# State copies moved ahead of a unit's loads, four plain items in place of two, partial sums added on VectorE

## The chip, the core and the metric

The kernel runs on one core of a Trainium2 chip: TensorE (PE), VectorE (DVE), ScalarE (ACT), GpSimd (POOL) and SyncE (SP), with 16 DMA engines. Its time is the device time of one execution in microseconds (us); a comparison uses the median of several.

## The reference

Two stages, all in float32 on the chip. First an mLSTM cell over `batch, heads, seq, head_dim = 4, 8, 768, 40`, then a two-layer block with tanh shrink (3072 tokens, 320 features, 2048 hidden):

```python
for t in range(S):
    m_new = np.maximum(f_gate[:, :, t] + m, i_gate[:, :, t])
    f_stab = np.exp(f_gate[:, :, t] + m - m_new);  i_stab = np.exp(i_gate[:, :, t] - m_new)
    C = f_stab * C + i_stab * outer(v_t, k_t);     n = f_stab * n + i_stab * k_t
    y[t] = sigmoid(o_gate[t]) * (C @ q_t) / np.maximum(np.abs(n @ q_t), 1.0)
x = y.transpose(0, 2, 1, 3).reshape(3072, 320)
h = x @ w_in            # 320 x 2048
out = (h - np.tanh(h)) @ w_out   # 2048 x 320
```

`w_in` and `w_out` arrive as 64-bit floats and are converted to float32 on the chip.

## The kernel before

**Units.** The cell works in 24 units of 128 tokens (4 batches, 6 chunks; unit `n` is chunk `n // 4` of batch `n % 4`). For a unit, `load_unit` fetches `kz`, `qz`, `v`, `k` and `o` through SP's queue. Units 0 to 5 are done in a first part whose order a planner (`Plan`, `plan_unit`, `plan_weights`) works out when the program is built; the conversion of the weights runs through it too (the first DVE operation of a weight block is a shift, `w_e<-w`; the list `begun` keeps these shifts in order). In this part TensorE fills its gaps with `awake` matmuls on a constant.

**Second part.** From unit 6 (`PLANNED`) on, each batch keeps its state in another layout, in halves; `in_halves(b)` makes it from the old one with seven small copies on SP's queue (`state<-state` in the profile). `block_turned` computes a unit's output transposed (`pT`), `turn_back` sends it through DRAM (`h_rows<-zt`, then `z_in<-h_rows`, both on SP's queue), and `gate_turned` gates it on DVE (`den<-z_in`, `o<-o,den`, two `ys`); `turn_by_store` turns it into the block's input (`yt`, `y_rows`, `xT`). `cell_slot` lays these steps out over two items for each unit, and at its begin issues the loads of the unit that follows.

**Items.** The two-layer block works on groups of 256 tokens (12 groups) times pairs of hidden blocks (8 for each group, `p`). An *item* is two pairs of one group. Its first product (`ph_up`) is computed either plainly (`up`: 8 matmuls of 128x128 by 256 columns, and the last 64 features) or with seven block products in place of eight (`up_in_seven`: 14 matmuls of 128 columns, copies of partial sums on ACT, sums of the weights from `sum_w_in`, sums of x from `sum_x`). The sums of the weights of pairs 0 to 3 lie where the partial outputs `part` of groups 0 to 2 lay. The polynomial in place of `h - tanh(h)` follows: squares on ACT (`z`, `q`), the rest on DVE (`gt<-ph_up,z`, `gt<-q,gt`). The two PSUM banks of `ph_up` are free for the next item when DVE has read them in `gt<-ph_up,z`. The second product (`pS`, 14 matmuls for each item, on sums `s` of `gt` and `wT` of w_out) lags one item: six of the 14 are held over and, in an item done in seven, are set between the stages of its first product. At a group's end `put_together(g)` adds the seven results (`a` on ACT, `ob`, `u` on DVE), and the next group's `pS` needs the banks it reads.

The planned part ends with item 6. Items 7 and 8 (group 0, pairs 4 to 7) are plain, items 9 and 10 (group 1) and 11 and 12 (group 2) are done in seven, as are all of groups 3 to 11 from item 13 on, but for the last. Groups 0 to 2 had their pairs 0 to 3 in the planned part; these are the `part` sums that `put_together` adds for `g < FIRST` (3).

**Order.** Every engine runs its instructions in the order in which they are written, and SP, ACT and POOL issue DMAs in that order as well. In the second part `merge` walks through an item's TensorE steps and puts the other steps in by their place (a number such as START + 2.33: a third of the way through the third item from START, item 7); `Clock.later` delays some of them. A `pause` in `cell_slot` is an empty step that moves the steps behind it later; a slot of unit pairs has 21 steps.

Of the kernel before, what the change touches and what calls it, by code (L numbers as in the profile page):

```python
# [55 lines left out]
OP = mybir.AluOpType  # L56
# [23 lines left out]
def kernel(  # L80
# [33 lines left out]
    V, A, SP, G = Pinned(nc.vector), Pinned(nc.scalar), Pinned(nc.sync), Pinned(nc.gpsimd)  # L114
# [168 lines left out]
    NG = NU // GT  # L283
    NP = NFF // 2
# [9 lines left out]
    FIRST, SPLIT = 3, 4  # L294
    NX = 6
    PLANNED, LEFT = 6, 3
# [58 lines left out]
    def load_unit(n, names=("kz", "qz", "v", "k", "o", "q2"), queue=SP, behind=(), crossed=False):  # L355
        c, b = divmod(n, B)
        t = ld.setdefault(n, {})
        t["crossed"] = crossed
        for name in names:
            if crossed and (name == "v" or name == "k" and n + B < NU):  # L360
                whole = load.tile([L, H if name == "v" else WIDE, D], FP, name=name, tag=name, bufs=3)
                t[name] = whole
                if name == "k":
                    G.memset(whole[:, H:], 0.0)
                load_crossed(whole[:, 0:H], (v if name == "v" else k)[b, c])
            elif name in ("kz", "qz"):
                t[name] = load.tile([128, HH, L], FP, name=name, tag=name, bufs=3)
                for i in range(2):
                    src = kT if name == "kz" else qT
                    dma = queue.dma_start(out=t[name][i * HALF:i * HALF + D], in_=src[b, c, :, i * HH:(i + 1) * HH])  # L370
                    if behind:
                        tc.add_manual_dep(dma.ins, behind[-1].ins.name, SYNC, reason="order of transfers")
            elif name == "k":
                if n + B < NU:
                    t["k"] = load.tile([L, WIDE, D], FP, name="k", tag="k", bufs=3)
                    queue.dma_start(out=t["k"].rearrange("p h d -> p (h d)"),
                                    in_=bass.AP(k.tensor, k[b, c].offset, [[H * D, L], [1, WIDE * D]]))
            elif name != "q2":
                src, bufs = {"v": (v, 3), "o": (o_gate, 4)}[name]
                t[name] = load.tile([L, H, D], FP, name=name, tag=name, bufs=bufs)  # L380
                queue.dma_start(out=t[name], in_=src[b, c])
            elif c:
                first = (n + 2) % 3 * len(TRIOS) * L
                t["q2"] = sums_in[0:TOP].rearrange("p a b -> p (a b)")[:, first:first + len(TRIOS) * L].rearrange("p (j t) -> p j t", t=L)
                for i in range(TRIO):
                    queue.dma_start(out=t["q2"][i * D:(i + 1) * D, 0:len(range(i, H, TRIO))], in_=qT[b, c, :, slice(i, H, TRIO)])
# [20 lines left out]
    two = const.tile([128, 1], FP, name="two")  # L407
# [30 lines left out]


    CHUNKS = (0, 2, NT)  # L440
    NS = NG * NP + 2 + (NG - FIRST) * NP // 2 - 1 + LEFT * (NP - SPLIT) // 2 - 2
    NW = NS + len(CHUNKS) - 1
    sums = const.tile([128, NW + 4 * NP], FP, name="sums")

# [10 lines left out]
    crossed = const.tile([L, NT - NEW, BH], FP, name="crossed")  # L455
# [17 lines left out]
    begun = []  # L473
# [24 lines left out]
    def gate_columns(c0, c1, bank):  # L498

        cs = slice(c0, c1)  # L500
        some = CHUNKS.index(c0)
        least = sums[:, NS + some:NS + some + 1]

# [137 lines left out]
    parts_of = [const.tile([L, GT, DM], FP, name=f"part{g}") for g in range(NP // 2)]  # L641
# [207 lines left out]
    def in_halves(b):  # L849


        c = NEW + (b < PLANNED % B)
        old, new = (state[b][(c + i) % 2].rearrange("p h d -> p (h d)") for i in (0, 1))
        for h in (0, 1, 2, 4, 5, 6, 7):
            i, j = divmod(h, HH)
            r = h % TRIO
            n = 2 if h == 0 else 1
            to, at = (x[:, first * D1:(first + TRIO * (n - 1) + 1) * D1].rearrange("p (h d) -> p h d", d=D1)[:, ::TRIO]
                      for x, first in ((new, j), (old, h)))
            SP.dma_start(out=to[i * HALF:i * HALF + D], in_=at[r * D:(r + 1) * D])  # L860
# [93 lines left out]
    def cell_slot(s, o):  # L954


        steps, pause = [], [(0.0, lambda: None)]
        if s is not None:
            if s + 1 < NU and s + 1 not in ld:
                load_unit(s + 1, ("kz", "qz", "v", "k", "o"), crossed=True)  # L960
            begin(s)
        def ready():
            prepare(s)
            G.memset(un[s]["wide"][:, H * D1:], 0.0)

        if o is None:
            return [(0.0, ready)]
        steps += 5 * pause
        if s is not None:
            steps.append((0.0, ready))  # L970
        steps += 5 * pause
        gates, behind = [], 5 * pause if o > PLANNED else 2 * pause
        if o == PLANNED:
            steps += 3 * pause
        steps.append((0.0, lambda: [gates.extend(gate_turned(o)), gates[0]()]))
        steps += [(0.0, lambda i=i: gates[i]()) for i in range(1, 4)]
        steps.append((0.0, lambda: turn_by_store(o)))
        return steps + behind
# [7 lines left out]
    gS, wT, pS, third = {}, {}, {}, {}  # L986
# [9 lines left out]
    def order_of(g):  # L996

        half = NP // 2
        return [0, half - 1, *range(half, NP), *range(1, half - 1)] if g == FIRST else list(range(NP))
# [72 lines left out]
    def put_together(g):  # L1072
        bank = pS[g]

        ob = mlp.tile([128, 5, HM], FP, name="ob", tag="ob")
        a = mlp.tile([128, HM], FP, name="a", tag="a", bufs=1)
        u = mlp.tile([128, 2, HM], FP, name="u", tag="u", bufs=1)

        def twice(t):
            return t.unsqueeze(1).to_broadcast([128, 2, HM])  # L1080

        def rest():
            V.tensor_tensor(out=ob[:, 0:5:4], in0=bank[0][:, 0:2], in1=twice(a), op=OP.add)
            V.tensor_tensor(out=u, in0=bank[1], in1=twice(ob[:, 4]), op=OP.add)
            V.tensor_tensor(out=ob[:, 3], in0=bank[1][:, 0], in1=u[:, 1], op=OP.add)
            V.tensor_tensor(out=ob[:, 1:3], in0=bank[2], in1=u, op=OP.add)
            if g < FIRST:
                both = ob[:, 0:2 * GT]
                (V if g in third else G).tensor_tensor(out=both, in0=both, in1=parts_of[g].rearrange("p t (two n) -> p (t two) n", two=2), op=OP.add)
            c, b = divmod(g * GT, B)  # L1090
            rows = out.rearrange("(b c t) n -> c t b n", b=B, c=NT)[c][:, b:b + GT]
            whole = ob[:, 0:4].rearrange("p (t two) n -> p t (two n)", two=2)
            if g >= FIRST or g in third:
                Clock.later("sent", 2.0, lambda: A.dma_start(out=rows, in_=whole))
            else:
                G.dma_start(out=rows, in_=whole)

        if g in third:
            return lambda: A.copy(out=a, in_=bank[0][:, 2]), rest
        A.copy(out=a, in_=bank[0][:, 2])  # L1100
        Clock.later("result", 0.5, rest)
# [301 lines left out]
    while sum(map(len, items)) < len(pairs):  # L1403
        x = sum(map(len, items))
# [11 lines left out]
    HOLD = 161.0478  # L1416
    FETCH = {(0, 1): 0.0000, (2, 1): 0.0000, (3, 0): 26.0323, (3, 1): 0.0000}
    APART = ()
    PLAIN = 2
    assert 3 * len(items) - START - PLAIN - 1 == NS  # L1420
    BETWEEN = 3
    BY_POOL = (1, 2, 3, 5, 6, 7,)
# [46 lines left out]
    of_tokens, of_states, exponentials, rows = {}, {}, [], []  # L1469
# [266 lines left out]
    for i, slot in enumerate(slots):  # L1736
        x0, x1 = (START + max(0, 2 * j - 1) for j in (i, i + 1))
        begins[x0].append((slot, x0, x1))
    for p, x in enumerate((4.05, 6.05, 8.05, 2.8, 0.5, 0.8, 1.1, 1.4)):
        spread_over([(0.0, lambda step=step: step()) for step in sum_w_in(p, G)], START + x, START + x + 0.25)  # L1740
    late = (4, 0.0, V), (5, 0.04, G), (6, 0.95, V), (7, 0.3, G)
    for p, x, E in (*late, *((p, x, G) for p, x in zip(order_of(FIRST)[:2] + order_of(FIRST)[-2:], (2.3, 2.7, 6.6, 7.5)))):
        spread_over([(0.0, lambda p=p, i=i, E=E: sums_at(p, E)[i][1]()) for i in range(4)], START + x, START + x + (0.1 if E is V else 0.3))
    for g, x in (1, 0.1), (2, 2.1):
        spread_over([(0.0, lambda g=g: sum_x(g, V))], START + x, START + x + 0.1)
    banks[:] = [name for name in ("b0", "b1") if name != third.setdefault("tag", "b0")]
    cross()
    load_unit(PLANNED, ("kz", "qz", "v", "k", "o"), crossed=True)
    in_halves(PLANNED % B)
    in_halves((PLANNED + 1) % B)  # L1750
    load_unit(PLANNED + 1, ("kz", "qz", "v", "k", "o"), crossed=True)
    in_halves((PLANNED + 3) % B)
# [148 lines left out]
    with tc.If(loaded[0] > 0):  # L1901
# [21 lines left out]
        for g in range(NG):  # L1923
# [30 lines left out]
            for tt in range(GT):  # L1954
                o = mlp.tile([128, 5, HM], FP, name="ob", tag="ob")[:, 0:2].rearrange("p two n -> p (two n)")
# [43 lines left out]
```

## Time and profile before

| | |
|---|---|
| Runs | 497.73, 501.45, 504.31 us; median 501.45 |
| The profiled execution | 498.91 us, of which the span from first to last instruction is 497.2 |
| Busy in the span | PE 97%, DVE 83%, ACT 54%, POOL 26% |
| Granted TensorE clock, mean | 0.997 |

The page gives busy times and groups of instructions; a timeline row is start, duration, engine, operation, tiles, count, and in brackets how long the engine sat idle before it and what ended that. A row of several instructions counts to the last one's end; a float32 matmul of this program stands as two records. Rows of the SP queue are the issue of DMAs, not their transfer.

### The profile page before, as it was taken

How to read it: one execution, taken by the hardware profiler on the slowest of the kernel's cores; microseconds unless marked ns; L12 is line 12 of the kernel's file. 1: busy time of each engine (PE TensorE's matmuls, PEld its weight loads, DVE VectorE, ACT ScalarE, POOL GpSimd, SP SyncE). 2: the span in 40 equal slices, each digit the busy share in tenths (PEclk: the TensorE clock that was granted, in tenths of full speed). 3: DMA queues.
4: the chain of work that ended last, by engine and by line, in shares of the span. 5: the costliest groups of instructions: out<-in, count | busy, mean ns of one | idle time of the engine just before them, and what ended most of it. 6: DMA issues, size and time to landing. Idle time of an engine off the chain costs nothing.

```text
span 497.2 us, 13817 instructions
## 1 busy us (share of the span) xinstructions
PE 483.0 (97%) x5208; PEld 432.8 (87%) x5208; DVE 411.2 (83%) x963; ACT 268.8 (54%) x729; POOL 129.0 (26%) x246
## 2 busy tenths in 40 slices
PE   9999999999999999999999999999999999999993
PEld 5778876788878999999999999999999999989983
DVE  4898979996999998997988888887887988776771
ACT  4888968634444544644644644644554644645440
POOL 5642325910735542111111111102102111111000
PEclk9999999999999999999999999999999999999998
DMA  7995494222634435545544444434525532410001
GB/s 224 297 263 181 74 203 139 73 69 46 122 92 120 88 92 114 114 90 118 107 95 102 96 105 106 93 91 109 101 67 113 110 82 38 90 37 1 26 2 32
DMA packets 143468, 51.26 MB, mean 103 GB/s; under 512 B 124004, under 2 KB 135716, under 8 KB 143396
## 3 DMA queue, kind: packets, MB, share of 16 engines
q1 hardware_dynamic: 135308, 31.70, 31.3%
q0 software_dynamic: 5424, 15.51, 10.5%
q10 hardware_dynamic: 2664, 3.11, 1.8%
q8 instruction: 43, 0.70, 0.6%
q14 instruction: 29, 0.24, 0.2%
HBM read 38.40 MB, written 11.60 MB: 101 GB/s over the span
## 4 chain that ended last, share of the span: by engine, by line
PE 60%; DVE 1%; issue 0%; ACT 0%
PE ph_up L129 27%; PE pS L129 27%; PE pT L129 3%; PE ps L129 2%; PE pc L129 1%; DVE gt L106 0%; DVE s L106 0%; DVE ob L106 0%; ACT ph_up L106 0%; DVE both L106 0%; DVE ys L106 0%; DVE u L106 0%; DVE yt L106 0%; PE count L129 0%
## 5 line engine op out<-in xcount | busy, mean ns | idle before, releaser
L129 PE MATMUL ph_up<-xT,w_in 64*64 64x256 f32 (+3 forms) x1324 | 155.0, 349 | 0.0
L129 PEld LDWEIGHTS ph_up<-xT,w_in 128*128 128x128 f32 (+2 forms) x1324 | 113.9, 162 | 17.2 <-issue 3.5
L106 ACT ACTIVATE z<-ph_up 128x256 f32<-128x256 f32 (+1 forms) x98 | 40.8, 417 | 106.1 <-PE ph_up L129 86.1
L106 POOL DMA_DIRECT2D xT<-y_rows x54 | 31.7, 592 | 230.5 <-DMA y_rows<-yt 230.5
L106 ACT COPY ph_up<-ph_up 128x256 f32<-128x256 f32 x117 | 41.9, 358 | 85.5 <-PE ph_up L129 54.7
L129 PE MATMUL pS<-wT,s 128*128 128x160 f32 x504 | 86.7, 300 | 0.0
L129 PEld LDWEIGHTS pS<-wT,s 128*128 128x128 f32 x504 | 72.9, 191 | 0.3 <-issue 0.3
L106 DVE SCALAR_TENSOR_TENSOR gt<-q,gt 128x512 f32<-128x512 f32 (+1 forms) x98 | 66.6, 686 | 4.6 <-ACT q L106 2.0
L106 ACT ACTIVATE q<-z,tiny 128x512 f32<-128x512 f32 (+1 forms) x98 | 68.9, 713 | 2.5
L106 DVE TENSOR_TENSOR both<-ph_up,cs 128x256 f32<-128x256 f32 x78 | 31.9, 419 | 30.8 <-PE ph_up L129 26.6
L129 PE MATMUL pS<-w_out,gt 128*128 128x160 f32 x336 | 56.9, 312 | 0.0
L129 PE MATMUL ph_up<-xT,sums_in 128*128 128x128 f32 x336 | 52.3, 278 | 3.6 <-DVE gt L106 3.0
L129 PEld LDWEIGHTS pS<-w_out,gt 128*128 128x128 f32 x336 | 46.8, 189 | 4.4 <-issue 1.9
L129 PEld LDWEIGHTS ph_up<-xT,sums_in 128*128 128x128 f32 x336 | 45.3, 191 | 6.0 <-issue 4.1
L129 PE MATMUL ph_up<-xT,part 128*128 128x128 f32 x288 | 44.9, 278 | 0.4 <-POOL ob L106 0.3
L106 DVE SCALAR_TENSOR_TENSOR gt<-ph_up,z 128x256 f32<-128x256 f32 (+1 forms) x98 | 41.1, 456 | 2.3 <-ACT z L106 2.2
L129 PEld LDWEIGHTS ph_up<-xT,part 128*128 128x128 f32 x288 | 38.8, 191 | 2.6 <-ACT ph_up L106 1.9
L106 DVE TENSOR_TENSOR s<-gt 128x256 f32<-128x256 f32 x84 | 33.6, 439 | 1.4
L129 PE MATMUL pS<-w_out,s 128*128 128x160 f32 x168 | 29.7, 299 | 0.0
L129 PE MATMUL pS<-wT,gt 128*128 128x160 f32 x168 | 29.7, 299 | 0.0
L129 PE MATMUL po<-w_out,gt 128*128 128x320 f32 x96 | 28.2, 440 | 1.2 <-DVE part L106 1.2
L106 DVE SCALAR_TENSOR_TENSOR gt<-both,z 128x512 f32<-128x512 f32 x39 | 29.3, 751 | 0.0
(140 smaller groups left out, 741.9 us busy)
## 6 DMA issues: line engine op xcount, KB each, us to landing
w<-in_moe_w_out POOLq DMA_DIRECT2D x8, 640.0 KB, 6.9
h_rows<-zt SPq DMA_DIRECT2D x72, 64.0 KB
z_in<-h_rows SPq DMA_DIRECT2D x72, 64.0 KB
w<-in_moe_w_in POOLq DMA_DIRECT2D x16, 256.0 KB, 6.3
kz<-in_kT SPq DMA_DIRECT2D x48, 80.0 KB
o<-in_o_gate SPq DMA_DIRECT2D x24, 160.0 KB
qz<-in_qT SPq DMA_DIRECT2D x44, 80.0 KB
y_rows<-yt SPq DMA_DIRECT2D x68, 40.0 KB
```

The costliest lines, as they stand in the source:

```text
L106: i = method(*args, **kwargs)
L129: return cls.keep(nc.tensor.matmul(*args, **kwargs))
```

## The change

1. `in_halves(2)` (seven copies) is issued ahead of the loads of unit 6, not behind them; and the `kz` and `qz` loads of unit 6 wait for the fourth-last shift of the weights (`behind=begun[-4:-3]`).
2. The gate steps of unit 6 move two of 21 steps later in their slot (START + 2.33 to START + 2.52).
3. `PLAIN` is 4, not 2: items 9 and 10 use `up`, and `sum_x(1)` is not needed. Two columns of `sums` fewer.
4. The sums of weights on POOL are made at other places; two sets of `wT` come earlier.
5. For groups 0 to 2 the addition of `part` in `put_together` runs on DVE in place of POOL, and the result is sent from ACT's queue, not POOL's.

```diff
-    NS = NG * NP + 2 + (NG - FIRST) * NP // 2 - 1 + LEFT * (NP - SPLIT) // 2 - 2
+    NS = NG * NP + 2 + (NG - FIRST) * NP // 2 - 1 + LEFT * (NP - SPLIT) // 2 - 4
...
-        gates, behind = [], 5 * pause if o > PLANNED else 2 * pause
+        gates, behind = [], 5 * pause if o > PLANNED else []
         if o == PLANNED:
-            steps += 3 * pause
+            steps += 5 * pause
...
-                (V if g in third else G).tensor_tensor(out=both, in0=both, in1=parts_of[g]..., op=OP.add)
+                V.tensor_tensor(out=both, in0=both, in1=parts_of[g]..., op=OP.add)
...
-            if g >= FIRST or g in third:
-                Clock.later("sent", 2.0, lambda: A.dma_start(out=rows, in_=whole))
-            else:
-                G.dma_start(out=rows, in_=whole)
+            Clock.later("sent", 2.0, lambda: A.dma_start(out=rows, in_=whole))
...
-    PLAIN = 2
+    PLAIN = 4
...
-    for p, x in enumerate((4.05, 6.05, 8.05, 2.8, 0.5, 0.8, 1.1, 1.4)):
+    for p, x in enumerate((4.05, 6.05, 8.05, 2.02, 1.2, 1.5, 2.2, 2.45)):
         spread_over([... for step in sum_w_in(p, G)], START + x, START + x + 0.25)
-    for p, x, E in (*late, *((p, x, G) for p, x in zip(order_of(FIRST)[:2] + order_of(FIRST)[-2:], (2.3, 2.7, 6.6, 7.5)))):
+    for p, x, E in (*late, *((p, x, G) for p, x in zip(order_of(FIRST)[:2] + order_of(FIRST)[-2:], (0.7, 0.95, 6.6, 7.5)))):
...
-    for g, x in (1, 0.1), (2, 2.1):
+    for g, x in ((2, 2.1),):
         spread_over([(0.0, lambda g=g: sum_x(g, V))], START + x, START + x + 0.1)
     cross()
-    load_unit(PLANNED, ("kz", "qz", "v", "k", "o"), crossed=True)
     in_halves(PLANNED % B)
+    load_unit(PLANNED, ("kz", "qz", "v", "k", "o"), behind=begun[-4:-3], crossed=True)
     in_halves((PLANNED + 1) % B)
```

More of the change, by code (lines that the diff above doesn't have):

```diff
@@ L1088, in rest @@
                 both = ob[:, 0:2 * GT]
-                (V if g in third else G).tensor_tensor(out=both, in0=both, in1=parts_of[g].rearrange("p t (two n) -> p (t two) n", two=2), op=OP.add)
+                V.tensor_tensor(out=both, in0=both, in1=parts_of[g].rearrange("p t (two n) -> p (t two) n", two=2), op=OP.add)
             c, b = divmod(g * GT, B)
```

## The prediction, made before the changed kernel ran

> **What bounds the kernel now.** I read the busy shares first, then TensorE's waits, then the timeline of the stage that the change touches.
>
> ```profile
> PE 483.0 (97%) x5208; PEld 432.8 (87%) x5208; DVE 411.2 (83%) x963; ACT 268.8 (54%) x729; POOL 129.0 (26%) x246
> ```
> ```profile
> 240.00:300.00 60.00, 60.00 (x752) 56.85 (x751) 52.87 (x131) 30.39 (x89) 10.13 (x24) 1.00 0.49 106
> ```
> ```profile
> PE ph_up L129 <- DVE gt L106: 3.0, 5, 0.9
> PE po L129 <- DVE part L106: 1.2, 1, 1.2
> ```
> ```profile
> PE ph_up L129 <- ACT ph_up L106: 0.6, 2, 0.3
> PE ph_up L129 <- POOL ob L106: 0.3, 1, 0.3
> ```
>
> TensorE is the bound, without a gap in the regular part (60.00 busy of 60 us). A gain can come only from its few waits: 3.0 us for the polynomial on VectorE and 1.2 us in the planned part. Everything added to TensorE's order is paid in full. All edits act between 66 and 190 us; what follows only shifts. These are the waits there, with what delays VectorE:
>
> ```profile
> 119.08 0.17 DVE L106 SCALAR_TENSOR_TENSOR den<-z_in,inv 128x8 f32<-128x8 f32 x1 [4.32 <-DMA z_in<-h_rows]
> ```
> ```profile
> 120.14 0.75 DVE L106 TENSOR_TENSOR both<-ph_up,cs 128x256 f32<-128x256 f32 x2
> ```
> ```profile
> 121.69 0.68 PE L129 MATMUL ph_up<-xT,sums_in 128*128 128x128 f32 x4 [0.56 <-DVE gt L106]
> ```
> ```profile
> 131.85 0.68 PE L129 MATMUL ph_up<-xT,sums_in 128*128 128x128 f32 x4 [0.61 <-DVE gt L106]
> ```
> ```profile
> 143.25 0.68 PE L129 MATMUL ph_up<-xT,sums_in 128*128 128x128 f32 x4 [0.90 <-DVE gt L106]
> ```
> ```profile
> 172.79 0.68 PE L129 MATMUL ph_up<-xT,sums_in 128*128 128x128 f32 x4 [0.36 <-DVE gt L106]
> ```
>
> VectorE stands 4.32 us at unit 6's gate, waiting for data that comes back through DRAM; item 9's reads of `ph_up` are behind it, so items 10, 11 and 12 start late by 0.56, 0.61 and 0.90, and item 15 by 0.36. The two waits for ACT's copies (0.3 each) stand inside items 10 and 12, the one put down to POOL (0.3) at item 13: 3.3 us in all.
>
> **Part A: copies first, loads behind.**
>
> ```profile
> 75.39 0.49 DVE L106 TENSOR_SCALAR w_e<-w 128x640 int32<-128x640 int32 x1 [2.99 <-DMA w<-in_moe_w_out]
> ```
> ```profile
> 76.54 0.90 DVE L106 TENSOR_TENSOR state<-pc,eT 120x328 f32<-120x328 f32 x2
> ```
> ```profile
> 78.08 0.48 DVE L106 TENSOR_TENSOR part<-po,part 128x320 f32<-128x320 f32 x1
> ```
> ```profile
> L106 POOL DMA_DIRECT2D w<-in_moe_w_out x3: 722/734/736, 68.0 to 80.3; - x3
> ```
> ```profile
> DMA to landing us min/median/max: 4.4/4.6/7.4
> ```
> ```profile
> 73.51 0.59 SPq L106 DMA_DIRECT2D o<-in_o_gate  x1
> 77.12 11.04 SPq L106 DMA_DIRECT2D state<-state  x14
> 88.20 0.87 SPq L106 DMA_DIRECT2D kz<-in_kT  x2
> ```
>
> The block of w_out issued at 68.0 takes 7.4 us to land; the two behind it take 4.4 and 4.6. Unit 6's loads are in flight beside the first (their last is issued at 73.51). With the loads behind the copies it should land at 68.0 + 4.5 = 72.5, and the shift at 75.39 comes 2.9 us earlier. The `part` addition at 78.08 with it, and TensorE's wait of 1.2 us for it goes: **-1.2** (from 0, if the loads are not what slows the block, to -1.2).
>
> The price is on SP's queue. The first copy needs unit 2's state, made at 76.54 behind that shift (so the explicit wait is always met by then and costs nothing of its own). Before, the copies started at 77.12, 1.7 after the shift; now at 74.2. But the loads of unit 6, which SP issued while it had nothing else to do, now stand behind the copies and in front of everything else: 5.8 us, as those of unit 7 take (88.20 to the next copies at 94.00).
>
> ```profile
> 94.00 10.82 SPq L106 DMA_DIRECT2D state<-state  x14
> ```
> ```profile
> 110.65 2.00 SPq L106 DMA_DIRECT2D h_rows<-zt  x4
> ```
>
> From 77.12 to 110.65 SP issues copies and loads almost without pause, so `h_rows` of unit 6 comes at 74.2 + 33.5 + 5.8 = 113.5 in place of 110.65, though its data are ready before either. From `h_rows` to the gate it took 119.08 - 110.65 = 8.4, so **the gate can begin at 121.9**, 2.8 later than before.
>
> **Part B: items 9 and 10 plain.** Plain and in seven:
>
> ```profile
> 475.16 4.68 PE L129 MATMUL ph_up<-xT,w_in 128*128 128x256 f32 x24
> 479.77 1.35 PE L129 MATMUL pS<-wT,s 128*128 128x160 f32 x8
> ```
> ```profile
> 211.13 0.89 PE ph_up L129 x8
> ```
> ```profile
> 214.10 2.81 PE ph_up L129 x32
> 216.91 1.11 PE pT L129 x48
> 218.02 0.60 PE pc L129 x16
> 218.61 2.37 PE pS L129 x16
> ```
>
> Plain takes 4.6 (start to start), in seven 0.89 + half of that for the middle four + 2.81 = 4.15: **+0.45** each on TensorE, though a plain item loses the small gaps between interleaved stages; I use the lengths whole, below. ACT loses four copies an item, VectorE two additions; that is spare time for VectorE, worth something only where it makes TensorE wait.
>
> **Part C: item 10 meets the gate.** Item 9 began at 110.85; 1.2 earlier is 109.65. Its first product 4.6 and unit 7's 1.7 (1.11 + 0.60) end at 116.0; 15 matmuls of `pS` at 2.37/8 make 4.4, and item 10 is wanted at 120.4. Its bank is free when VectorE has done item 9's first `gt<-ph_up,z`, which could be at about 117.5. But `merge` sets the gate by the costs that the code gives its steps: those of item 9 ahead of the polynomial are 1.72 + 1.9 + 1.72 = 5.34 of 9.99, and the later gate, at 0.524 x 9.99 = 5.23, falls just ahead of it, the next gate step ahead of the first read. VectorE waits for `z_in` until 121.9, then den and `o` take 1.06 (119.08 to 120.14), the read 0.65: 123.7. **Wait of 3.3 us** where there were 0.56 and 0.3.
>
> **Part D: the change of group in item 10.** In seven, the last matmuls of group 0 stood between stages, and `put_together(0)` was done beside the last stage. A plain item has no such places: after its first product come five matmuls of group 0 and at once group 1's, which need the banks.
>
> ```profile
> 107.79 0.85 PE L129 MATMUL ps<-qz,kz 40*64 40x128 f32 x32
> ```
> ```profile
> 108.07 0.60 ACT L106 ACTIVATE z<-ph_up 128x512 f32<-128x512 f32 x1 [3.02 <-PE ph_up L129]
> ```
> ```profile
> 109.22 1.33 ACT L106 ACTIVATE q<-z,tiny 128x512 f32<-128x512 f32 x2
> ```
> ```profile
> 124.99 0.30 ACT L106 COPY a<-pS 128x160 f32<-128x160 f32 x1
> ```
>
> Plain item 8 shows ACT busy until 2.76 after the product's end (107.79 to 110.55). In item 10 the product ends at 123.7 + 4.5 = 128.2; scores 0.8 and five matmuls 1.5 bring TensorE to 130.5. ACT gets to `a` after 2.76 and 0.6 of unit 8's column and gate: `a` until 131.9, `ob` 0.48 on VectorE, and `pS` of group 1 at 132.6. **Wait of 2.1** (from 0, if ACT is done in time, to 3). Eight more matmuls: item 11 begins at **135.0, against 131.85 before: +3.1**.
>
> **Part E: behind it.** VectorE has caught up by then: it has about 2 us of work less (two items, one each), so the 0.90 and 0.3 of item 12 go. The additions of `part` are VectorE's now:
>
> ```profile
> L106 DVE SCALAR_TENSOR_TENSOR w_in<-w,w_e x8: 811/819/1150, 17.2 to 84.6; 128x640 int32<-128x640 int32 x8
> ```
> ```profile
> 133.46 2.50 DVE L106 SCALAR_TENSOR_TENSOR gt<-both,z 128x512 f32<-128x512 f32 x1
> ```
> ```profile
> 171.24 0.74 DVE L106 TENSOR_TENSOR both<-ph_up,cs 128x256 f32<-128x256 f32 x2
> ```
> ```profile
> 133.88 1.53 POOL L106 TENSOR_TENSOR ob<-ob,part 128x640 f32<-128x640 f32 x1
> ```
> ```profile
> 171.06 1.67 POOL L106 TENSOR_TENSOR ob<-ob,part 128x640 f32<-128x640 f32 x1 [2.03 <-issue]
> ```
>
> An operation of this shape costs 0.8 there. The first POOL addition stood beside a `gt` of 2.50 (0.69 elsewhere), the third beside one of the usual length: the first move gives VectorE 1 us back, the third costs 0.8 just ahead of item 15's reads, which were late already. I take 0.8 left of the 1.9 that items 12 to 15 waited: **-1.1** (from -1.9 to +1.0). [...]
>
> POOL's other moves cost nothing that I can see: its queue stands still from 101 to 123 before its next DMA, which is room for the 4 us of sums that come earlier. If VectorE is slowed by them, item 9 starts up to 1 us late.
>
> **Sum.** +3.1 at item 11 (in it -1.2, the gaps of items 10 and 11, the longer products, and the two new waits), -1.1 behind: **+2.0 us**. The profiled execution took 498.91 (span 497.2 and 1.7 around it): 500.9 on its scale. It lies 2.5 below the median 501.45 of three runs that spread from 497.73 to 504.31; on the median's scale **503.4**. 2%, about what a measurement of this kernel can tell from no change, is 10 us: I forecast no change by that measure, leaning to slower.
>
> **Rivals.**
> 1. *Item 9's reads are not held by the gate* (the other side). Place: the gate of unit 6. If `z_in` lands before 118.6, TensorE finds the bank free, 3.3 goes, and the sum is -1.3: 500.1; with D at 0 as well, -3.4: 498.0. It decides from `h_rows` issued before 110.2. For: copies cost 0.79 each when SP is beside other traffic, perhaps less alone. Against: the copies cannot start before 74, and 39 us follow.
> 2. *The block of w_out lands no earlier*, since w_in's rest and the tiny pieces of `crossed` slow it. Then the change does not do what its first part says: A is 0, the copies start at 77.1, the gate at 124.8, item 10 wanted at 121.6 starts at 126.6: 5.0 in place of 3.3. Sum 2.0 + 1.2 + 1.7 = +4.9: 506.3.
> 3. *TensorE's clock drops in C.*
>
> ```profile
> 488.88 0.71 PE L129 MATMUL pS<-w_out,s 128*128 128x160 f32 x4
> ```
> ```profile
> 494.00:496.00 2.00, 0.00 (x0) 0.00 (x0) 0.00 (x0) 0.00 (x0) 0.00 (x0) 0.52 0.02 4
> ```
>
> After the last matmul (489.6) the granted clock falls at about 494.1, after 4.5 us of rest; 1.2 us (the largest gap inside) left it at 1.00. A wait of 3.3 lies between. [...]
>
> **How the numbers follow.** Forecast (+0.5 to +3.5) 0.45; rival 1 0.25; rival 2 0.18; rival 3 0.05; none of these 0.07. The range takes rival 1's lower end, 498.0, and rival 2 with a little of the runs' own spread, 508.0. A change over 10 us needs two unseen things at once: faster 0.02, slower 0.04, within 0.94.
>
> **What would show it.** A: the shift at 75.39 comes near 72.5 and TensorE's 1.2 is gone; `h_rows` of unit 6 near 113.5. B: 24 and 32 records of 256 columns in items 9 and 10. C: VectorE's wait at `den` grows from 4.32 to about 6, and TensorE waits some 3 us for `gt` near 120. D: TensorE waits about 2 us at the first `pS` of group 1, for `ob`. E: no wait at item 12, about 1 us near item 15. I am wrong if SP is faster than its rows say, if the order of the steps on VectorE is not the one I walked through, or if ACT is done earlier in D.

## The result, and the profile after

The changed kernel took 502.36 us (median of 22 runs, 500.73 to 507.81) beside 498.59 of the kernel before on the same chip (22 runs): ratio 1.0092, 95% interval 1.0065 to 1.0119. That is 0.9% slower, within the 2% of no change, as forecast. The profiled execution took 501.97 (span 500.1) against 498.91 (span 497.2): +3.06 where +2.0 was forecast. By the medians the difference is +3.8; the sums below go by the profiled executions.

One thing is needed to read the times below: the runs of one kernel can lie some 5 us apart, and four of the profiled executions lost about that much in their first 20 us, whatever the edit (the last section shows it), and the text says which.

The page's busy shares are within two points of those of before, and TensorE's waits are others: one of 5.1 us and one of 1.6 in place of many short ones.

```profile
PE 484.2 (97%) x5176; PEld 434.2 (87%) x5176; DVE 409.4 (82%) x956; ACT 265.3 (53%) x717; POOL 121.8 (24%) x240
```
```profile
PE ph_up L129 <- DVE gt L106: 5.7, 2, 5.1
PE pS L129 <- DVE ob L106: 1.6, 1, 1.6
```

**A.** The timeline of VectorE, TensorE and SP. The block of w_out, issued at 67.4 with none of unit 6's loads beside it, lands in 5.8 us (7.4 before, 4.5 forecast). The shift comes 2.2 us earlier (73.19 for 75.39), and the row of 20 `po` matmuls at 74.89 runs without the 1.22 of before (the first row here): item 9 begins at 109.27, 1.58 earlier. The copies begin 2.2 earlier, and `h_rows` 5.6 later (116.24 for 110.65):

```profile
78.62 3.50 PE L129 MATMUL po<-w_out,gt 128*128 128x320 f32 x12 [1.22 <-DVE part L106]
```
After:

```profile
73.19 0.49 DVE L106 TENSOR_SCALAR w_e<-w 128x640 int32<-128x640 int32 x1 [1.39 <-DMA w<-in_moe_w_out]
```
```profile
74.89 5.65 PE L129 MATMUL po<-w_out,gt 128*128 128x320 f32 x20
```
```profile
109.27 1.89 PE L129 MATMUL ph_up<-xT,w_in 128*128 128x256 f32 x8
```
```profile
74.89 5.55 SPq L106 DMA_DIRECT2D state<-state  x7
80.48 0.87 SPq L106 DMA_DIRECT2D kz<-in_kT  x2
```
```profile
99.00 10.83 SPq L106 DMA_DIRECT2D state<-state  x14
```
```profile
113.27 2.24 SPq L106 DMA_DIRECT2D k<-in_k  x3
115.56 0.58 SPq L106 DMA_DIRECT2D o<-in_o_gate  x1
116.24 1.99 SPq L106 DMA_DIRECT2D h_rows<-zt  x4
```

**C and D.** VectorE stands 8.54 us at `den`, reads item 9's bank behind it, and TensorE stands 5.10. Then item 10's first product takes 7.18 us (125.39 to the scores at 132.57) where a plain one takes 4.6: the granted clock is 0.50 from about 123.9 to 130.7. The last columns of the windows are clock, DMA share, GB/s:

```profile
123.59 0.17 DVE L106 SCALAR_TENSOR_TENSOR den<-z_in,inv 128x8 f32<-128x8 f32 x1 [8.54 <-DMA z_in<-h_rows]
```
```profile
124.65 0.68 DVE L106 SCALAR_TENSOR_TENSOR gt<-ph_up,z 128x512 f32<-128x512 f32 x1
```
```profile
119.31 0.98 PE L129 MATMUL pS<-wT,s 128*128 128x160 f32 x6
125.39 7.36 PE L129 MATMUL ph_up<-xT,w_in 128*128 128x256 f32 x32 [5.10 <-DVE gt L106]
132.57 0.85 PE L129 MATMUL ps<-qz,kz 40*64 40x128 f32 x32
```
```profile
136.55 1.35 PE L129 MATMUL pS<-w_out,gt 128*128 128x160 f32 x8 [1.58 <-DVE ob L106]
```
```profile
139.03 0.61 PE L129 MATMUL ph_up<-xT,sums_in 128*128 128x128 f32 x4
```
```profile
120.40:123.80 3.40, 0.00 (x0) 0.00 (x0) 0.17 (x2) 0.00 (x0) 0.00 (x0) 1.00 0.72 113
123.80:124.00 0.20, 0.00 (x0) 0.00 (x0) 0.17 (x1) 0.00 (x0) 0.00 (x0) 0.73 0.61 87
124.00:130.60 6.60, 5.21 (x12) 4.21 (x13) 5.57 (x14) 0.00 (x0) 0.64 (x2) 0.50 0.55 113
130.60:130.80 0.20, 0.20 (x2) 0.13 (x1) 0.00 (x0) 0.00 (x0) 0.20 (x1) 0.71 0.79 203
```

**E.** Item 11 begins 7.18 late (139.03 for 131.85); then the lag shrinks: item 12 begins without a wait at 149.15 (+5.90), item 13 at 157.91 (+4.80), item 15 at 177.78 (+4.99, a wait of 0.61), and the last matmuls are at 492.46 (+3.58). The first row is item 13 of before, the others are after.

```profile
153.11 0.68 PE L129 MATMUL ph_up<-xT,part 128*128 128x128 f32 x4 [0.30 <-POOL ob L106]
```
```profile
149.15 0.61 PE L129 MATMUL ph_up<-xT,sums_in 128*128 128x128 f32 x4
```
```profile
157.91 0.61 PE L129 MATMUL ph_up<-xT,part 128*128 128x128 f32 x4
```
```profile
177.78 0.68 PE L129 MATMUL ph_up<-xT,sums_in 128*128 128x128 f32 x4 [0.61 <-DVE gt L106]
```
```profile
492.46 0.71 PE L129 MATMUL pS<-w_out,s 128*128 128x160 f32 x4
```

### The profile page after: what moved, and what is told of

It reads as the page before. It is cut to its first block, busy times and chain, and to the rows that moved or that the text cites. A ratio compares the mean times of both kernels' runs of the same rounds, so it can differ in the third digit from the quotient of the medians.

```text
span 500.1 us, 13734 instructions
## 1 busy us (share of the span) xinstructions
PE 484.2 (97%) x5176; PEld 434.2 (87%) x5176; DVE 409.4 (82%) x956; ACT 265.3 (53%) x717; POOL 121.8 (24%) x240
## 4 chain that ended last, share of the span: by engine, by line
PE 83%; SPq 6%; DVE 4%; DMA 3%; issue 1%; POOL 1%; ACT 0%; DVEq 0%; ACTq 0%
PE ph_up L129 36%; PE pS L129 31%; SPq L106 6%; PE po L129 3%; PE pT L129 3%; PE ps L129 3%; PE ph L129 2%; PE pc L129 2%; PE awake L129 1%; DMA h_rows<-zt 1%; DVE gt L106 1%; POOL wT L106 1%; PE px L133 0%; DMA w_out<-in_i_gate 0%; DMA k<-in_k 0%
## 5 line engine op out<-in xcount | busy, mean ns | idle before, releaser
L129 PE MATMUL ph_up<-xT,w_in 64*64 64x256 f32 (+3 forms) x1324 | 161.6, 353 | 5.1 <-DVE gt L106 5.1
L129 PEld LDWEIGHTS ph_up<-xT,w_in 128*128 128x128 f32 (+2 forms) x1324 | 118.7, 164 | 24.3 <-DVE gt L106 5.3
L106 ACT COPY ph_up<-ph_up 128x256 f32<-128x256 f32 x111 | 39.6, 357 | 92.1 <-PE ph_up L129 61.4
L129 PE MATMUL ph_up<-xT,sums_in 128*128 128x128 f32 x304 | 46.6, 276 | 0.6 <-DVE gt L106 0.6
L106 DVE SCALAR_TENSOR_TENSOR gt<-ph_up,z 128x256 f32<-128x256 f32 (+1 forms) x98 | 42.3, 469 | 2.3 <-ACT z L106 2.2
L129 PEld LDWEIGHTS ph_up<-xT,sums_in 128*128 128x128 f32 x304 | 41.2, 191 | 1.2 <-issue 0.8
L106 DVE SCALAR_TENSOR_TENSOR gt<-both,z 128x512 f32<-128x512 f32 x37 | 25.3, 684 | 0.0
```

Source lines behind the costliest of these rows:

```text
L106: i = method(*args, **kwargs)
L129: return cls.keep(nc.tensor.matmul(*args, **kwargs))
```

## Experiments

Experiments e1 to e4 ran beside the kernel before at 499.03 us (median), as did e5 to e8; e9 to e12 ran beside 499.43. Parts 2 and 4 were not run alone.

**e1: the gate moved, nothing else.** After, with the gate steps of unit 6 set at START + 3.80.

```diff
         if o == PLANNED:
-            steps += 5 * pause
+            apart = [(0.0, lambda: [gates.extend(gate_turned(o)), gates[0]()])]
+            apart += [(0.0, lambda i=i: gates[i]()) for i in range(1, 4)]
+            apart.append((0.0, lambda: turn_by_store(o)))
+            spread_over(apart, START + 3.8, START + 3.95)
+            return steps + 10 * pause
```

> The changed kernel with unit 6's gate steps set at START + 3.80, behind put_together(0) in item 10, and nothing else. If the gate's wait is the cause: z_in lands near 123.6 as before and nobody stands behind it, so TensorE's 5.1 us wait before item 10 and the halved clock (item 10's product 7.2 in place of 4.5) both go, item 11 begins near 131.5, and the kernel ends about 7 us earlier: some 495 us, faster than before the change. If the cost lies in the plain items and the group change themselves, TensorE still waits and item 11 still begins after 135; the kernel stays near 502.

497.53 us, ratio 0.9976 (0.9931 to 1.0021); five of its ten runs lie between 494.56 and 495.95, the others above 499. Profiled 494.56, 7.4 less than after.

```profile
119.94 4.64 PE L129 MATMUL ph_up<-xT,w_in 128*128 128x256 f32 x32
```
```profile
128.39 1.35 PE L129 MATMUL pS<-w_out,gt 128*128 128x160 f32 x8 [1.58 <-DVE ob L106]
```

Item 10 starts at 119.94 without a wait, its product takes 4.47 (scores at 124.41), though `h_rows` is as late as in after (116.05). So `z_in` cost TensorE nothing but through VectorE's order: item 9's reads stood behind the gate. The 1.58 of part D is there as before.

**e2: part 1 undone.** After, with the loads of unit 6 ahead of the copies and no `behind`.

```diff
-    in_halves(PLANNED % B)
-    load_unit(PLANNED, ("kz", "qz", "v", "k", "o"), behind=begun[-4:-3], crossed=True)
+    load_unit(PLANNED, ("kz", "qz", "v", "k", "o"), crossed=True)
+    in_halves(PLANNED % B)
```

> The changed kernel with its first part undone: unit 6's loads ahead of the copies again, without the explicit wait. If SP's queue is what makes the gate late: the shift waits for the w_out block until 75.4 again and TensorE's 1.2 us wait near 78 is back, h_rows of unit 6 goes out near 110.7 and z_in lands near 119; item 10 is wanted at 121.6 and starts there or at most 0.5 later, at a full clock; so about 5 us less than the changed kernel, some 497. If the copies' place does not matter, den still waits until 123 and the kernel stays near 502.

497.12 us, ratio 0.9944 (0.9894 to 0.9994); profiled 495.73.

```profile
111.06 2.00 SPq L106 DMA_DIRECT2D h_rows<-zt  x4
```
```profile
119.12 0.17 DVE L106 SCALAR_TENSOR_TENSOR den<-z_in,inv 128x8 f32<-128x8 f32 x1 [2.19 <-DMA z_in<-h_rows]
```

`h_rows` is back at 111.06 and `den` at 119.12; the wait at item 10 is gone (it starts at 122.01), the 1.5 for `part` at 78 is back. Parts 2 to 5 alone bring 3.2 us by the profiles.

**e3: part 1 alone**, that exchange of lines the other way in the kernel before.

> The kernel before with the first part alone: copies ahead of unit 6's loads and the explicit wait, the gate at START + 2.33, items 9 and 10 in seven. If SP's queue makes the gate late: the 1.2 us wait near 78 goes, h_rows near 116, z_in lands near 123.5, and as the gate stands ahead of item 9's additions TensorE waits for item 10 from 119.9 until about 125, with the clock falling: 3 to 6 us slower than before, 502 to 505. If only the plain items make the changed kernel slow, this one is 1 us faster than before, 497.

504.80 us, ratio 1.0108 (1.0031 to 1.0185); profiled 502.98.

```profile
126.46 1.19 PE L129 MATMUL ph_up<-xT,sums_in 128*128 128x128 f32 x4 [6.77 <-DVE gt L106]
```
```profile
137.40 0.61 PE L129 MATMUL ph_up<-xT,sums_in 128*128 128x128 f32 x4
```

`h_rows` at 115.71, a wait of 6.77, and the clock at 0.50 from 124.3 to 131.2. With e2: part 1, which takes TensorE's 1.2 at 78 away, is the whole slowdown, with or without plain items. Item 11 begins 5.55 later than before (137.40), and by the last matmul (492.96) the kernel is 4.08 behind: 1.5 us come back with no plain item and no addition moved.

**e4: the clock kept up.** After, with 12 `awake` matmuls on a constant ahead of item 10's product.

```diff
         news = new
+        if x == START + 3:
+            dense.insert(0, (0.0, lambda: stream(ps_a.tile([128, 512], FP, name="awake", tag="a0"), 12)))
```

> The changed kernel with 12 matmuls on a constant (128x512, bf16, some 0.22 us each, 2.6 us) in front of item 10's product: work that computes nothing, to keep TensorE busy in the wait. If the 2.7 us by which item 10's product is longer come from the clock that falls in the idle time: TensorE's idle time falls to 2.5 us, item 10 still begins at 125.4, but its product takes 4.5 and the kernel is 2.7 us faster than the changed one, near 499.5. If the product is long for another reason (VectorE or ACT holding it), nothing changes and it stays near 502.

501.14 us, ratio 1.0030 (0.9998 to 1.0062); this profiled execution (505.54) lost 5.4 us at the start.

```profile
125.59 2.75 PE L129 MATMUL awake<-diag 128*128 128x512 bf16 x12
130.95 4.75 PE L129 MATMUL ph_up<-xT,w_in 128*128 128x256 f32 x32 [2.61 <-DVE gt L106]
135.52 0.85 PE L129 MATMUL ps<-qz,kz 40*64 40x128 f32 x32
```

TensorE is as late (2.75 of constants and 2.61 of waiting make 5.36), the clock stays at 1.00, and the product takes 4.57 in place of 7.18. The halved clock was worth 2.6 us at item 10, on top of the wait. Not all of it reaches the end: the median is 1.2 us below after's, where 2.7 were expected, item 15 waits 1.25 for 0.61, and the three lowest of ten runs (499.52 to 499.69) are where the expectation had it.

**e5: part B alone**, in the kernel before.

```diff
-    PLAIN = 2
+    PLAIN = 4
-    for g, x in (1, 0.1), (2, 2.1):
+    for g, x in ((2, 2.1),):
```

> The kernel before with part B alone: items 9 and 10 plain (and the sums of x of group 1, which only an item in seven needs, not made). Copies, loads, gate and additions stay as before. Theory (the plain items cost little; it was the late z_in that cost): h_rows of unit 6 stays near 110.7 and den near 119.1, its wait near 4.3; VectorE frees item 9's bank about 1.8 after den, 120.9, and item 10 is wanted at about 121.9, so TensorE does not wait there. It waits about 1.6 for ob at the first pS of group 1 (part D) and no more at items 12 and 13. Profiled execution 495 to 497, against 498.91 before. Rival (a plain item costs 0.45 and D 1.6, with nothing given back): the waits at items 12 to 15 stay, 500 to 501. Second rival: the gate in its old place keeps VectorE from item 9's reads and item 10 waits 1 us or more: 497.5 to 498.5.

500.54 us, ratio 1.0022 (0.9978 to 1.0066); profiled 497.29, the four lowest of ten runs 496.72 to 497.29.

```profile
123.19 4.75 PE L129 MATMUL ph_up<-xT,w_in 128*128 128x256 f32 x32 [1.08 <-DVE gt L106]
131.74 1.35 PE L129 MATMUL pS<-w_out,gt 128*128 128x160 f32 x8 [1.58 <-DVE ob L106]
```
```profile
134.20 0.61 PE L129 MATMUL ph_up<-xT,sums_in 128*128 128x128 f32 x4
```

The expectation's theory missed the 1.08: the second rival's mechanism is there, near the size it gave, and the profiled time lies between the two. In e2 `den` comes at the same time (119.12, here 119.07) and item 10 does not wait. By VectorE's rows, unit 7's `zt` and `state` operations stand ahead of the gate there and behind it here, so that item 9's reads begin at 120.17 there and at 122.45 here: the later gate of part 2 would do this, though it was not run alone. Item 11 begins 2.35 later than before (134.20), and by the last matmul the kernel is 1.48 ahead (487.40): 3.8 us come back behind item 11 with no addition moved.

**e6: the additions alone** (part 5), in the kernel before.

```diff
-                (V if g in third else G).tensor_tensor(out=both, in0=both, in1=parts_of[g]..., op=OP.add)
+                V.tensor_tensor(out=both, in0=both, in1=parts_of[g]..., op=OP.add)
...
-                G.dma_start(out=rows, in_=whole)
+            Clock.later("sent", 2.0, lambda: A.dma_start(out=rows, in_=whole))
```

> The kernel before with the two additions of part on VectorE in place of GpSimd, and ACT's queue sending out, and nothing else. Theory as predicted in part E: the wait of 0.30 at item 13 goes, the long gt of 2.50 at 133.46 becomes about 0.7, 0.8 each is added to VectorE; sum between -1.0 and +0.5, profiled execution 498 to 499.4. Rival (the additions are cost alone): items 12, 14 or 15 wait 0.8 more each, 500 to 500.5. If the additions are what gave after its gain behind item 11 (4.3 from there to the end), it is 495 to 496.5.

498.81 us, ratio 1.0011 (0.9969 to 1.0053); profiled 498.22.

```profile
129.76 0.97 DVE L106 TENSOR_TENSOR ob<-ob,part 128x640 f32<-128x640 f32 x1
130.65 1.49 DVE L106 TENSOR_TENSOR vs<-v,crossed 128x320 f32<-128x320 f32 x1
```
```profile
133.62 0.68 PE L129 MATMUL ph_up<-xT,sums_in 128*128 128x128 f32 x4 [2.35 <-DVE gt L106]
```

The edit moves three additions (POOL's at 133.88, 151.32 and 171.06 of before), not the two of which the expectation speaks. It is neutral in all, as part E had it, but not by its route: the addition ahead of item 11's reads makes its wait 2.35 for 0.61, a drop of the clock follows (0.50 for 3.41 us, in the last section), and the waits of items 12 and 13 go.

**e7: one plain item less, the gate of e1.** `PLAIN = 3`, `sum_x(1)` kept.

> The changed kernel with the gate of unit 6 at 3.80 to 3.95 behind the start, as in the run with the gate moved, and with only item 9 plain (item 10 in seven, the sums of x of group 1 made). Theory: no wait for gt at item 10; the wait of 1.58 for ob at the change of group goes, as in seven there is other work between; item 10 is 0.45 shorter: 2 us less than the run with the gate moved (494.56 profiled), 492 to 493. Rival: VectorE's added work (two additions an item, the sums of x) makes items 10 and 11 wait 0.3 to 0.6 each as before: 493.5 to 495.

495.62 us, ratio 0.9922 (0.9882 to 0.9962); the profiled execution (499.43) lost 5.4 at the start, the lowest runs are 494.19 to 494.31.

```profile
155.58 0.68 PE L129 MATMUL ph_up<-xT,part 128*128 128x128 f32 x4 [1.19 <-DVE gt L106]
```

The 1.58 of part D is gone, so it does come with a plain item at the change of group. But VectorE, with more to do, is late at item 13: the rival's mechanism and its size held, at another item than it named. The lowest run is no more than 0.4 below e1's, which is 494.56.

**e8: SP's order.** After, with the loads of unit 8 issued behind `h_rows` and `z_in` of unit 6.

```diff
-            if s + 1 < NU and s + 1 not in ld:
+            if s == PLANNED + 1:
+                late = [(0.0, lambda: load_unit(s + 1, ("kz", "qz", "v", "k", "o"), crossed=True))]
+            elif s + 1 < NU and s + 1 not in ld:
...
             steps.append((0.0, ready))
+            if s == PLANNED + 1:
+                steps += late
```

> The changed kernel with one move on SP: the eleven loads of unit 8 are issued behind h_rows and z_in of unit 6, not ahead of them. Nothing else. Theory (SP's queue made z_in late): h_rows at 109.9 to 110.5 in place of 116.24, den near 117.7 with a wait under 3.5, item 9's bank free at 119.5, before item 10 is wanted at 120.3: TensorE's 5.10 goes, its clock stays at 1.00, profiled execution 494 to 495, 7 less than after's 501.97. If the transfer is slower for other reasons (traffic of copies), den comes after 120 and 1 to 3 us of the wait stay: 496 to 499. If the wait has nothing to do with SP's queue: 501 to 502. Rival on the other side: unit 8's loads, 5.5 later, are late for its scores and item 11 or 12 waits: 497 or more.

495.78 us, ratio 0.9895 (0.9844 to 0.9946). The profiled execution (499.01) lost 5.2 at the start: the product that begins at 70.28 in after begins at 75.47 here.

```profile
115.13 2.05 SPq L106 DMA_DIRECT2D h_rows<-zt  x4
```
```profile
122.58 0.17 DVE L106 SCALAR_TENSOR_TENSOR den<-z_in,inv 128x8 f32<-128x8 f32 x1 [2.34 <-DMA z_in<-h_rows]
```
```profile
125.31 4.64 PE L129 MATMUL ph_up<-xT,w_in 128*128 128x256 f32 x32
```

Less 5.2, `h_rows` is at 109.9, `den` at 117.4, and item 10 starts at 120.1 without a wait: the expected numbers. The clock is 1.00 from 116 to 144. Eleven DMA issues standing in front of four made the 5.10 and the clock's drop.

**e9: the same move in the kernel before.**

> The kernel before with one move on SP: the eleven loads of unit 8 are issued behind h_rows and z_in of unit 6, not ahead of them. Nothing of the change itself. Theory (SP's queue, by way of z_in, sets the waits of items 10 to 12 before as well): h_rows at 105 to 108 in place of 110.65, den between 113.5 and 116.5 with a wait under 2 in place of 4.32, and the waits of items 10, 11 and 12 (0.56, 0.29, 0.61, 0.90, 0.29) go, all or most: 496 to 497 for an execution like the profiled one of 498.91. Rival (VectorE is simply full there, whatever z_in does): the waits shrink by less than 1 us in all, 498 to 499.

494.84 us, ratio 0.9912 (0.9871 to 0.9952); profiled 495.92.

```profile
108.11 1.98 SPq L106 DMA_DIRECT2D h_rows<-zt  x4
```
```profile
141.10 0.68 PE L129 MATMUL ph_up<-xT,sums_in 128*128 128x128 f32 x4 [0.16 <-DVE gt L106]
143.33 0.71 PE L129 MATMUL ph_up<-xT,sums_in 128*128 128x128 f32 x4 [0.29 <-ACT ph_up L106]
```

`h_rows` is only 2.5 earlier, and VectorE no longer waits at `den` (115.60): of 2.65 at items 10 to 12, 0.45 is left.

**e10: e8 with three plain items; e11: e8 with part 1 undone.**

> The changed kernel with unit 8's loads behind h_rows and z_in of unit 6, and with only item 9 plain (item 10 in seven, the sums of x of group 1 made). Theory: TensorE's 5.10 at item 10 and its 1.58 at the change of group go both: 0.5 to 1.5 below the same move with four plain items, lowest times 492 to 493.3 against 493.41 there. Rival (as with the gate moved, VectorE's added work gives the gain back in waits for gt at items 12 to 15): the same to 1 us more, lowest times 493.4 to 494.5.

> The changed kernel with its first part undone (loads of unit 6 ahead of the copies) and unit 8's loads behind h_rows and z_in of unit 6. Theory: the 1.2 to 1.5 that TensorE waits for part at 78 is back, and no wait at item 10 either way, since it had none with the first part undone alone: 495 to 496 for an undisturbed start, as there (495.73), and 1.2 more than with the first part kept. If z_in earlier frees VectorE further, the 0.40 at item 15 goes too: 494.5 to 495.

e10: 495.47 us, ratio 0.9925 (0.9887 to 0.9963), profiled 494.62, lowest 493.14; its waits at items 13 and 15 (1.08 and 1.02) take back most of what D gave, as the rival said; the lowest run is just inside the theory's range, 0.27 below e8's 493.41. e11: 496.20, ratio 0.9924 (0.9890 to 0.9957), lowest 494.60; its profiled execution (499.59) lost 5 at the start, so its wait for `part` (0.25) can't be set beside the others.

**e12: the gate moved, in the kernel before.** The edit of e1, with nothing else of the change.

> The kernel before with one move: the gate steps of unit 6 are set at 3.80 to 3.95 behind the start, behind the reads of item 9 in VectorE's order, not ahead of them. Nothing else of the change. Theory (what cost TensorE was that item 9's reads stand behind the wait for z_in): no wait at den, TensorE's 0.56 and 0.29 at item 10 go, and with VectorE 4 us ahead those of items 11 and 12 (0.61, 0.90, 0.29) shrink to under 1 us in all: 496 to 497 for an execution like the profiled one of 498.91. Rival: the gate's 2.9 us of VectorE work then meet items 10 and 11 and the waits only move: 498 to 499.

494.24 us (six runs, 493.61 to 494.94), ratio 0.9883 (0.9843 to 0.9922); profiled 494.87.

```profile
119.01 0.75 DVE L106 SCALAR_TENSOR_TENSOR gt<-ph_up,z 128x256 f32<-128x256 f32 x2
```
```profile
130.67 0.16 DVE L106 SCALAR_TENSOR_TENSOR den<-z_in,inv 128x8 f32<-128x8 f32 x1
```

Item 9's reads are done at 119.76, the gate comes at 130.67 and waits for nothing. From item 9 to item 13 it is 37.83 us (112.07 to 149.90), against 42.26 before (110.85 to 153.11): 4.4, where the marked waits were 2.95. The view has no idle time for the other 1.5: it counts TensorE busy for 39.32 us there before and for 37.83 here, on the same items. Each of the six waits costs some 0.25 us beside its mark (an estimate, 1.5 divided by 6): from the last `pS` row to item 10 it is 1.53 us before and 0.81 here, 0.72 for a marked wait of 0.56, because rows overlap at their ends where TensorE runs on (in before the `pS` row at 130.00 lasts 0.71 and the next begins at 130.54, 0.17 ahead of its end). This version beats the kernel before by more than its interval, and with that the changed one. e8, e9 and e10 have lowest times within 0.5 us of its 493.61; which of the four is best isn't settled.

## Why the prediction was right, and where not

The sum was +2.0 and came out at +3.06. That the two are so near is luck: it is two errors of 3 to 4 us each with opposite signs, about +4 at item 11 and -3 behind it. The mechanism of A, C and D was right.

- **A**, the gain: right in kind, and past the end of its range (1.58 at item 9; 0 to -1.2 was forecast). The shift came at 73.19, not 72.5, because the block, though issued 0.6 earlier, took 5.8 us to land, not 4.5. The gain is larger than the mark of 1.22, as e12 shows of such waits.
- **A**, the price: right in kind, undersized. `h_rows` came at 116.24, not 113.5: copies 0.7 later, and 41.35 us from there to `h_rows` in place of 39.3, mostly since v of unit 7 and k of unit 8 took 2.54 and 2.24 on SP where I had carried over 1.6 and 1.7. The way to the gate was 7.35, not 8.4. The gate began at 123.59, not 121.9.
- **B**: e1's item 10 lasts 10.92 with 1.58 of waiting, e7's in seven 8.77: +0.57 for a plain item (0.45 forecast), in which some 0.2 belongs to the wait beside its mark.
- **C**: the order walked through was the one on the chip; the wait was 5.10, not 3.3, by the gate's 1.7. Item 10 was wanted at 120.29 (120.4 forecast).
- **Rival 3** came on top, with the 2.6 us of e4. The failed step is its chance of 0.05. The rows of before had the clock at 1.00 beside a wait of 1.2 us and down after a rest of 4.5, and do not say on which side a wait of 3.3 lies. The wait's own range should have counted too: it came out at 5.10. And 3.3 was no safe length by what the last section shows: the clock fell behind a rest of 2.35 in e6, and stayed at 1.00 behind 2.61 in e4.
- **D**: 1.58 for 2.1, as `a` was done 3.4 us behind the product's end, not 3.7, and TensorE came to the wait 0.1 later; seen unchanged in e1, e2, e4, e5 and e8, and gone in e7.
- Item 11 began 4.0 later than forecast: 1.7 of C and 2.6 of the clock, less 0.5 of D, and 0.2 of small gaps.
- **E** was mis-sized the other way: 7.18 to 3.58 is -3.6, and 0.7 more behind the last matmul (why is open), against -1.1. e5 shows nearly all of it (3.8) with the additions left on POOL, so it is not the additions. TensorE's lateness alone, which lets VectorE catch up, gives 1.5 (e3, 5.55 late); e5, only 2.35 late, gives 3.8, so the two plain items give at least 2.3 of it. e12 gains 3.0 behind item 11 with neither (0.90 ahead at 130.95, 3.88 at 485.00). What counts is that VectorE is not behind, and plain items are one way to that. I had counted marked waits alone (1.9), and left out the wait of 0.58 near 442 and what each wait costs beside its mark.
- **Rivals 1 and 2**: neither came. The block did land earlier without the loads: 5.8 us in after and 5.4 in e3, against 7.4 before and 7.9 in e2. e8 shows rival 1's condition: `h_rows` at 109.9, just ahead of the 110.2 named, and no wait.

## What to carry to other kernels

SP issued its DMAs here in the order of the program: with eleven loads ahead of it `h_rows` came at 116.24, with them behind it at 109.9 (e8, less 5.2). So, before a load is moved, add up what then stands between it and the one transfer on which an in-order engine waits. When an engine waits for data from DRAM, look first at what stands behind the waiting instruction; moving the wait behind it (e12, 494.24) gave at least as much here as making the data earlier (e9, 494.84), and more than making the work smaller (e5, 500.54). And a long wait of TensorE (2.35 us in e6) has to be priced together with the time at half the clock that may follow (3.41 us there, 6.83 in after).

## What the runs showed of the hardware

**The clock.** In after it fell at 123.89 and came back at 130.72 (from the 0.73 and 0.71 of the two short windows above): 6.83 us at 0.50. In e3 it was as long, from 124.32 to 131.15 (0.81 and 0.62 in the windows of 0.2 us from 124.20 and 131.00), and in e6 it was 3.41, half of that:

```profile
134.40:134.60 0.20, 0.20 (x5) 0.20 (x4) 0.20 (x2) 0.20 (x1) 0.20 (x1) 0.95 0.62 236
134.60:137.80 3.20, 3.20 (x15) 3.20 (x14) 3.10 (x8) 1.44 (x4) 1.61 (x3) 0.50 0.51 125
137.80:138.00 0.20, 0.20 (x2) 0.20 (x2) 0.20 (x2) 0.00 (x0) 0.00 (x0) 0.52 0.06 19
```

It fell there at 134.58, a microsecond after TensorE had gone on, and the rest before it was only 2.35 us (131.27 to 133.62), while e4's rest of 2.61 (128.34 to 130.95) left it at 1.00. So the length of a wait alone doesn't decide. Nor was the time from the start of a rest to the fall always the same: 3.31 us in e6, 3.60 in after (from 120.29), 4.63 in e3 (from 119.69), and 2.77 behind the last matmul of after (493.17 to 495.94, where the 0.2 us from 495.80 have 0.86). And the clock did not come back when TensorE went on: in after matmuls ran from 125.39, 5.33 us of them at 0.50, and in e3 from 126.46, 4.69 us. What sets the place of a fall and its length, these runs don't show.

**The start.** In four of the profiled executions (e4, e7, e8, e11) TensorE's rows took nearly twice as long until about 17 us, though the rows of granted clock read 1.00 there (0 to 24 us in e7 and e8): the same nine matmuls, 2.12 us in after and 3.92 in e4 (3.85 in e11).

```profile
9.67 2.12 PE L129 MATMUL awake<-diag 128*128 128x512 bf16 x9
```
```profile
13.46 3.92 PE L129 MATMUL awake<-diag 128*128 128x512 bf16 x9
```

In e4, e7 and e8 the product that begins at 70.28 in after begins 5.2 to 5.4 us later, which is more than the change is worth. What decides it was not tried.
